# Two decode layers streamed through SBUF: slots of 512 KB in place of 1 MB, half of one head's values kept, second-layer queries taken head by head

## The chip, the cores and the metric

One core of one Trainium2 chip. The time is the device time of one execution in microseconds (us). Ratios are the mean time of one kernel's fast runs over that of the other's in the same rounds, so they are not quite the ratio of the medians that are quoted beside them. The kernel before was run again beside every group of kernels; its median moved between 1197.8 and 1201.7 us from chip to chip, so kernels of different groups are compared by their ratios to it.

In the profiles PE is TensorE, PEld its weight load, DVE VectorE, ACT ScalarE, POOL GpSimd, and SP the engine that issues the loads. The granted clock (PEclk) is the share of TensorE's full clock that a stretch had. An eviction is a copy of TensorE's results into SBUF.

## The reference

Two layers with the same weights and the same caches. Each is grouped-query attention of one new token over 4096 cached positions (16 query heads on 8 key/value heads of width 256), then a small MLP block, for a batch of 8:

```python
B, Sq, D = 8, 1, 448
Hq, Hkv, Sk, Dh = 16, 8, 4096, 256
# k_cache, v_cache: (B, Hkv, Sk, Dh) bf16, 134 MB each
x = x + _A_ref(_layernorm(x), A_k_cache, A_v_cache, A_wq, A_wo)
x = x + _B_ref(_layernorm(x), B_w1, B_w2, B_w3, B_w4)
x = x + _A_ref(_layernorm(x), A_k_cache, A_v_cache, A_wq, A_wo)   # the same caches again
x = x + _B_ref(_layernorm(x), B_w1, B_w2, B_w3, B_w4)
```

Keys and values of one pair (batch element, head) are 2 MB each. Layer 2 of a batch element cannot start before all eight heads of layer 1 and the MLP are done. Whatever is not still in SBUF by then is read from HBM a second time.

## The kernel before

It keeps the keys of five heads of a batch element (10 MB) from layer 1 to layer 2, and streams everything else through the rest of its 15 slots of 1 MB. Keys are transposed on TensorE; scores, softmax and values follow; the values of a pair come one pair later (LAG). A small list scheduler in the kernel takes each operation's estimated duration and fixes the order of every engine's instructions ahead of time. On the chip each engine follows that order.

```python
HALVES = 15          # slots of 1 MB
KEEP_K = 5           # heads whose keys stay
KEEP_V = 0
...
def load_half(cache, b, h, half):
    i = free_slots.pop(0)
    slot_n[i] += 1
    src = cache[b, h].rearrange("(m s) d -> m (s d)", m=P)[:, half * 4096:(half + 1) * 4096]
    dma("kv", slot_ap(i, 0, 4096), src, 1 << 20, slot_sem[i], 16 * slot_n[i],
        [("s", i, j) for j in range(4)], loads[0])
...
# in pair(): per half j: load K, 4 transposes (TensorE) with evictions, 2 groups of score matmuls;
# the slot is free after the last score of the half; V likewise after its last value matmul
```

Between the layers of batch element b stands `mid`: MLP, norm, and the queries of layer 2. The first head's queries are computed and copied alone, the other seven together:

```python
groups = [[heads[0]], heads[1:]]
for gr in groups:
    for h in gr:  pe(... q_mms of head h ...)          # 16 matmuls a head
    for h in gr:  dv(... copy psC to q2T of head h ...)
```

The order of pairs around it, which hides part of `mid` behind two filler heads of the next batch element:

```python
for b in range(B):
    mid(b, l2_heads[0], l2_heads + free_heads)
    layer1(b + 1, free_heads[:NFILL])        # 2 filler heads, beside mid
    layer2(b, l2_heads[:2])                  # heads 7 and 6: keys already in SBUF
    layer1(b + 1, free_heads[NFILL:])
    layer2(b, l2_heads[2:])
    layer2(b, free_heads)
    layer1(b + 1, kept_heads)                # (edge cases cut)
```

## Time and profile before

| | before |
|---|---|
| median of 4 runs | 1197.81 us |
| span of the profiled run | 1196.5 us |
| bytes moved by all queues | 466.5 MB |
| TensorE busy | 84% |

Three lines of the page of the kernel before: the span; each engine's busy time with its share and instructions; and the load queue with its packets, MB and share of 16 engines' span.

```profile
span 1196.5 us, 46172 instructions
PE 1005.6 (84%) x21301; PEld 861.9 (72%) x21301; DVE 509.1 (43%) x1632; ACT 274.3 (23%) x847; POOL 97.9 (8%) x270
q1 hardware_dynamic: 69344, 463.58, 96.1%
```

The load queue is busy nearly all the time, so the loads are the first suspect. Where are they not at full rate? Below are windows of the kernel before: first ten microseconds of the plateau, then stretches of 8 us from the end of layer 1 of the fourth batch element (at 547.4 us). The columns are the stretch, its length, the busy time of each engine with its instructions, the granted TensorE clock, the DMA share, and GB/s.

```profile
core 0: us, PE busy (x) PEld busy (x) DVE busy (x) ACT busy (x) POOL busy (x), PEclk, DMA share, GB/s
480.00:490.00 10.00, 9.32 (x183) 8.09 (x182) 4.73 (x12) 3.58 (x9) 0.75 (x2) 1.00 1.01 419
547.40:555.40 8.00, 8.00 (x160) 7.91 (x158) 5.43 (x19) 2.93 (x5) 0.00 (x0) 1.00 0.99 393
555.40:563.40 8.00, 8.00 (x191) 7.63 (x188) 4.59 (x17) 1.94 (x7) 0.75 (x2) 1.00 0.84 289
563.40:571.40 8.00, 5.82 (x205) 5.17 (x201) 3.20 (x23) 0.65 (x4) 0.75 (x2) 0.91 0.95 355
571.40:579.40 8.00, 7.34 (x164) 6.08 (x165) 2.24 (x8) 1.23 (x5) 0.75 (x2) 0.66 0.86 314
579.40:587.40 8.00, 7.28 (x185) 6.57 (x182) 4.03 (x11) 1.73 (x6) 0.75 (x2) 1.00 1.00 416
```

On the plateau the loads run at 415 to 420 GB/s. After the layer change they sag to 289 GB/s, come back, and sag again to 314. In the first two stretches of 8 us TensorE is busy all of the time, and so, nearly, is its weight load (PEld): 7.91 and 7.63 us. The Trainium skill (Perfetto Trace Analysis, Identifying the Most-Contended Engine) calls matmul busy time a poor measure of how near TensorE is to its limit and asks for its arithmetic rate and the weight-load share; in these two stretches busy time and weight load say the same. The second sag is not the same case: there TensorE is busy 7.34 us and its weight load 6.08, at a granted clock of 0.66. The load queue's own waits in the kernel before, between 122 and 140 us (layer change): who issues, whom it waited for, total, times, longest.

```profile
engine line waited for: us in total, times, longest us
SPq L441 <- PE psS L697: 14.6, 3, 6.7
SPq L441 <- PE psS L737: 4.1, 2, 3.7
```

The queue waits for slots that score (L697) and value matmuls (L737) have yet to free. From the chain of work that ended last, around that change, as start, duration, what:

```profile
138.53 0.43 PE psC L594 x16
138.96 0.54 PE psW L775 x20
139.50 2.83 PE psC L594 x107
142.33 2.29 issue
144.61 0.31 PE psC L594 x5
144.92 2.57 PE psS L697 x64
147.49 1.81 PE psS L737 x32
```

L594 is a query matmul, L697 a score, L775 the output projection. The scores of the first second-layer head (x64) stand behind all 128 query matmuls and an idle of 2.29 us marked "issue" (TensorE waited for nothing that the profile names).

From the packets of a trace I count the bytes that arrive in each stretch, and call *loss* the time by which they fall short of 417.4 GB/s, the plateau of the kernel before. The stretches are set by the moment X at which VectorE writes the last sum of layer 1 of a batch element (the layer change). "Ahead" is X-24 to X, "first dip" X to X+24, "late" X+24 to X+64; each is summed over the eight layer changes. "Rest" is the plateau between them. The time of the bytes and all losses add up to the span by construction:

```
           span = bytes at 417.4 + start + ahead + first dip + late + rest + end
before   1196.5 =        1117.7  +   7.1 +   0.2 +      38.9 + 13.5 +  0.4 + 18.7
```

So 52.6 us are lost around the eight layer changes, 6.6 us at each.

### The profile page before, as it was taken

To read this page: it belongs to the slowest core of one execution; us is meant where nothing else is said; L and a number is where in the kernel's file an instruction comes from. 1 tells how busy PE (TensorE), PEld (TensorE's weight loads), DVE (VectorE), ACT (ScalarE), POOL (GpSimd) and SP (SyncE) were. 2 spreads that over 40 slices of the span, in tenths; PEclk is the share of its full clock that TensorE was granted. 3 is DMA by queue.
4 is the path that set the end of the run, shared out by engine and by line. 5 is a ranking of instruction groups with operands and counts; after the bars stand their busy time and mean duration, and the time that the engine had idled before them with its cause. 6 is when DMAs were issued, how large, how long until landed. Compare 5 with 4: busy or idle time off the path is not lost.

```text
span 1196.5 us, 46172 instructions
## 1 busy us (share of the span) xinstructions
PE 1005.6 (84%) x21301; PEld 861.9 (72%) x21301; DVE 509.1 (43%) x1632; ACT 274.3 (23%) x847; POOL 97.9 (8%) x270
## 2 busy tenths in 40 slices
PE   4878889889898887999789797888888888789787
PEld 4766877778677776777677686776877677678665
DVE  3433435444344443445344343444434453345333
ACT  0222213221132211332123211232223221132121
POOL 0000010000110011000110001000010000100110
PEclk9998889998899988999899988999889997899888
DMA  9999899999999999999999989999999999999893
GB/s 348 409 398 418 320 413 416 417 414 348 417 416 418 385 372 417 418 416 359 390 416 417 418 325 401 417 415 418 346 417 417 417 399 350 417 417 366 345 415 155
DMA packets 69536, 466.52 MB, mean 390 GB/s; under 512 B 7120, under 2 KB 13152, under 8 KB 13664
## 3 DMA queue, kind: packets, MB, share of 16 engines
q1 hardware_dynamic: 69344, 463.58, 96.1%
q8 instruction: 167, 2.74, 0.9%
q14 instruction: 25, 0.20, 0.0%
HBM read 463.54 MB, written 0.01 MB: 387 GB/s over the span
## 4 chain that ended last, share of the span: by engine, by line
PE 53%; DMA 34%; DVE 5%; issue 4%; SPq 3%; POOL 1%; ACT 0%
DMA kv<-in_A_v_cache_dram 20%; PE psT L805 18%; PE psS L697 14%; DMA kv<-in_A_k_cache_dram 14%; PE psS L737 8%; PE psW L775 4%; SPq L441 3%; PE psT L941 2%; DVE oS L751 2%; DVE oS L749 2%; PE psC L640 1%; PE psS L759 1%; PE psC L594 1%; PE psC L534 1%; PE psC L616 1%
## 5 line engine op out<-in xcount | busy, mean ns | idle before, releaser
L805 PE MATMUL psT<-ident_f,kv 128*128 128x128 f32 x2816 | 383.4, 284 | 11.4 <-DMA kv<-in_A_k_cache_dram 8.3
L805 PEld LDWEIGHTS psT<-ident_f,kv 128*128 128x128 f32 x2816 | 315.3, 145 | 25.6 <-DMA kv<-in_A_k_cache_dram 13.7
L813 DVE COPY kv<-psT 128x512 f32<-128x512 f32 x379 | 260.4, 691 | 171.2 <-PE psT L805 168.4
L814 ACT COPY kv<-psT 128x512 f32<-128x512 f32 x325 | 190.3, 586 | 517.9 <-PE psT L805 517.6
L737 PE MATMUL psS<-kv,pT 128*2 128x256 bf16 x4096 | 167.4, 289 | 45.2 <-DMA kv<-in_A_v_cache_dram 38.5
L697 PE MATMUL psS<-q2T,kv 128*128 128x48 bf16 x4096 | 145.6, 192 | 23.0 <-issue 22.8
L717 ACT ACTIVATE pT<-psS,nb 128x32 bf16<-128x32 f32 x256 | 73.2, 296 | 365.0 <-DVE nb L711 365.0
L697 PEld LDWEIGHTS psS<-q2T,kv 128*128 128x128 bf16 x4096 | 133.7, 103 | 31.7 <-issue 29.4
L697 PE MATMUL psS<-q1T,kv 128*128 128x48 bf16 x4096 | 143.2, 183 | 5.4 <-issue 4.9
L697 PEld LDWEIGHTS psS<-q1T,kv 128*128 128x128 bf16 x4096 | 130.1, 97 | 22.8 <-issue 17.6
L737 PEld LDWEIGHTS psS<-kv,pT 128*2 128x2 bf16 x4096 | 78.9, 85 | 75.5 <-DMA kv<-in_A_v_cache_dram 45.0
L709 POOL PARTITION_ALL_REDUCE gm<-pm x128 | 45.4, 354 | 893.5 <-DVE pm L707 845.6
L707 DVE TENSOR_REDUCE pm<-psS 128x2 f32<-128x64 f32 x128 | 28.7, 224 | 182.9 <-PE psS L697 182.2
L941 PE MATMUL psT<-ident_b 128*128 128x256 bf16 x614 | 100.3, 288 | 1.9 <-issue 1.9
L759 PEld LDWEIGHTS psS<-sel,oS 128*128 128x128 bf16 x512 | 23.9, 98 | 105.6 <-DVE oS L751 103.8
L775 PEld LDWEIGHTS psW<-oT,wo_sb 128*128 128x128 bf16 x2560 | 79.9, 97 | 23.2 <-DVE oT L765 11.9
L759 PE MATMUL psS<-sel,oS 128*128 128x2 bf16 x512 | 32.4, 167 | 74.7 <-DVE oS L751 67.7
L775 PE MATMUL psW<-oT,wo_sb 128*128 128x24 bf16 x2560 | 90.0, 183 | 6.0 <-issue 5.0
L749 DVE CAST oS<-psS 128x256 bf16<-128x256 f32 x128 | 54.1, 423 | 74.7 <-PE psS L737 72.3
L941 PEld LDWEIGHTS psT<-ident_b 128*128 128x128 bf16 x614 | 49.6, 100 | 22.9 <-issue 17.6
L722 POOL PARTITION_ALL_REDUCE Db<-rs x128 | 51.1, 399 | 173.4 <-ACT pT L717 173.4
L751 DVE TENSOR_TENSOR oS<-psS,oS 128x256 bf16<-128x256 f32 x128 | 54.3, 424 | 3.3
(83 smaller groups left out, 461.2 us busy)
## 6 DMA issues: line engine op xcount, KB each, us to landing
kv<-in_A_v_cache_dram SPq DMA_DIRECT2D x256, 1024.0 KB, 17.9
kv<-in_A_k_cache_dram SPq DMA_DIRECT2D x176, 1024.0 KB, 20.9
wo_sb<-in_A_wo_dram SPq DMA_DIRECT2D x1, 3584.0 KB, 32.9
wq_sb<-in_A_wq_dram SPq DMA_DIRECT2D x3, 1024.0 KB, 11.3
w_sb<-in_B_w_dram SPq DMA_DIRECT2D x1, 1568.0 KB, 23.8
w_sb<-in_B_w_dram SPq DMA_DIRECT2D x3, 448.0 KB, 24.4
wqx_sb<-in_A_wq_dram SPq DMA_DIRECT2D x2, 256.0 KB, 14.9
w3x_sb<-in_B_w_dram SPq DMA_DIRECT2D x2, 112.0 KB, 20.1
```

The lines of the kernel that those rows point to most:

```text
L697: last = t.matmul(ps[:, 2 * i:2 * i + 2 * REP], a[:, c:256:2], bcast(rhs(c), REP, 1), start=(c == 0), stop=(c == 1))
L717: return a.activation(pT[nr][:, :, :].rearrange("p i j -> p j i")[:, jj, :], sview[:, jj, :], ACT.Exp, bias=nb[nr][:, jj:jj + 1], scale=IN ...
L722: plan.op("pool", lambda gp: gp.partition_all_reduce(Db[nr][:, :], rs[nr][:, :], P, RO.add), 0.5, "sum", rd=[("rs", nr, 0), ("rs", nr, 1)] ...
L737: last = t.matmul(ps[g4:g4 + 2, PV0:PV0 + DH], pT[nr][:, i, :], slot_ap(s_, s * 256, 256), start=(i < 4), stop=(i >= 28), skip_group_check ...
L749: plan.op("dve", lambda v: v.tensor_copy(oS[:, 0, :], po), 0.36, "o", rd=[("pv", par, x) for x in range(4)], wr=["oS0"], banks=[bk], prio=hi)
L751: plan.op("dve", lambda v: v.tensor_tensor(oS[:, 1, :], po, oS[:, 0, :], ALU.subtract), 0.36, "o", rd=["oS0"] + [("pv", par, x) for x in r ...
L759: last = t.matmul(ps[:, PV1 + 2 * c:PV1 + 2 * c + 2], oS[:, w, c * P:(c + 1) * P], sel[:, :], start=(w == 0), stop=(w == 1))
L775: last = t.matmul(psW[:, mt * YW:(mt + 1) * YW], dup(wo_sb, 2 * (2 * h + j) + c, mt), bcast(oT[nr][:, c, j:j + 1], YW, 1), start=(k == 0), ...
L805: last = t.transpose(psT[bank][:, s * P:(s + 1) * P], src, ident_f[:, :])
L813: return e.tensor_copy(dst, psT[bank][:, :])
L814: return e.copy(dst, psT[bank][:, :])
L941: last = t.matmul(psT[bank][:, 256 * i:256 * i + 256], ident_b[:, :], bcast(ident_b[:, :], 2, 1), start=True, stop=True)
```

## The change

The intent: read less (half of one head's values stays, 1 MB per batch element), use the slots in finer pieces where they are scarce and in bigger loads where many are free, and let the first layer-2 scores start earlier. The diff is shortened; words in brackets and comments are mine.

```diff
-HALVES = 15
+QUARTERS = 30
-KEEP_V = 0
+KEEP_V = 2
+MARGIN4, MARGIN2 = 16, 8
+QFIRST = 8
...
+    def grab(n):      # 4, 2 or 1 neighbouring slots, oldest first, if enough others are free
+        rank = {q: k for k, q in enumerate(free_slots)}
+        for k, margin in ((4, MARGIN4), (2, MARGIN2), (1, 0)):
+            if k > n:
+                continue
+            best = None
+            for q in range(0, QUARTERS - k + 1, k):
+                if all(q + x in rank for x in range(k)):
+                    r = max(rank[q + x] for x in range(k))
+                    if r < len(rank) - margin and (best is None or r < best[0]):
+                        best = (r, q)
...
+    def load(cache, b, h, units):    # one DMA and one semaphore for each group of slots grabbed
...
-        for j in range(2):           # halves of 1 MB
+        for u in range(4):           # quarters of 512 KB: loaded, transposed, scored, freed
...
-            for gr in groups: (queries of a group, then its copies)
+        for h in heads:
+            second_queries(b, h, None)      # 16 matmuls, then the copy, head by head
...
-        mid(b, l2_heads[0], l2_heads + free_heads)
+        order2 = l2_heads + free_heads
+        mid(b, order2[:QFIRST])             # QFIRST = 8: all heads, so none is left to spread
+        q_todo[b] = order2[QFIRST:]
```

The edit also gives the scheduler another estimate of a load's duration: the same for 1 MB (2.38 us), 1.22 in place of 1.19 us for 512 KB, 4.70 in place of 4.77 for 2 MB.

More of the change, by code (lines that the diff above doesn't have):

```diff
@@ L346, in bass_interleave_layers__gqa_block_cached__mixer_s_mlp__decode_kernel @@
     plan = Plan()
-    half_b = 8192
-    high0 = 229344 - HALVES * half_b
-    kv = nc.alloc_sbuf_tensor_at("kv", [P, HALVES * half_b // 2], bf, offset=high0)
+    high0 = 229344 - QUARTERS * 4096
+    kv = nc.alloc_sbuf_tensor_at("kv", [P, QUARTERS * 2048], bf, offset=high0)
     cursor = [16512]
@@ L420, in bass_interleave_layers__gqa_block_cached__mixer_s_mlp__decode_kernel, with slot_ap @@
     psW = nc.alloc_psum_tensor("psW", [P, 512], f32)
-    def slot_ap(i, a, n):
-        return kv[:, i * 4096 + a:i * 4096 + a + n]
+    def slot_ap(q, a, n):
+        return kv[:, q * 2048 + a:q * 2048 + a + n]
     sems = {e: nc.alloc_semaphore(f"s_{e}") for e in ("pe", "dve", "act", "pool")}
-    slot_sem = [nc.alloc_semaphore(f"s_slot{i}") for i in range(HALVES)]
-    slot_n = [0] * HALVES
+    slot_sem = [nc.alloc_semaphore(f"s_slot{i}") for i in range(QUARTERS)]
+    slot_n = [0] * QUARTERS
     def bcast(ap, shape, axis):
@@ L435, in bcast, with dma @@
         return bass.AP(tensor=ap.tensor, offset=ap.offset, ap=dims)
-    RATE = 440e3
-    def dma(name, dst, src, nbytes, sem, val, wr, at):
-        plan.op("sp", lambda eng: eng.dma_start(dst, src), nbytes / RATE, name, wr=wr, prio=at,
+    FASTER = 1.05
+    def dma(name, dst, src, nbytes, sem, val, wr, at, row=8192):
+        us = nbytes / 16 / 26.88e3 + nbytes / row / 16 * 0.008
+        plan.op("sp", lambda eng: eng.dma_start(dst, src), us / FASTER, name, wr=wr, prio=at,
                 dma=(sem, val))
@@ L450, in bass_interleave_layers__gqa_block_cached__mixer_s_mlp__decode_kernel @@
     loads = [0]
-    def load_half(cache, b, h, half):
-        i = free_slots.pop(0)
-        slot_n[i] += 1
-        src = cache[b, h].rearrange("(m s) d -> m (s d)", m=P)[:, half * 4096:(half + 1) * 4096]
-        dma("kv", slot_ap(i, 0, 4096), src, 1 << 20, slot_sem[i], 16 * slot_n[i],
-            [("s", i, j) for j in range(4)], loads[0])
-        loads[0] += 1
-        return i
-    free_slots = list(range(HALVES))
+    def grab(n):
[9 more added lines that the diff above has]
+                        best = (r, q)
+            if best is not None:
+                got = [best[1] + x for x in range(k)]
+                for q in got:
+                    free_slots.remove(q)
+                return got
+        raise AssertionError("no slot")
+    def load(cache, b, h, units):
+        out = {}
+        units = list(units)
+        while units:
+            run = 1
+            while run < len(units) and units[run] == units[0] + run:
+                run += 1
+            got = grab(run)
+            n, q, u = len(got), got[0], units[0]
+            slot_n[q] += 1
+            src = cache[b, h].rearrange("(m s) d -> m (s d)", m=P)[:, u * 2048:(u + n) * 2048]
+            dma("kv", slot_ap(q, 0, n * 2048), src, n << 19, slot_sem[q], 16 * slot_n[q],
+                [("s", x, j) for x in got for j in range(2)], loads[0], row=n * 4096)
+            sizes[n] = sizes.get(n, 0) + 1
+            loads[0] += 1
+            for x in range(n):
+                out[u + x] = got[x]
+            units = units[n:]
+        return out
+    sizes = {}
+    free_slots = list(range(QUARTERS))
     YB = ["yb"]
@@ L657, in bass_interleave_layers__gqa_block_cached__mixer_s_mlp__decode_kernel @@
     store = {}
+    KEPT_K = {h: range(4) for h in range(HKV - KEEP_K, HKV)}
+    KEPT_V = {HKV - 1: range(4 - KEEP_V, 4)}
     done = {}
@@ L678, in pair, with sc @@
             qk = [("q2", b, h)]
-        ks = [None, None] if kept_k is None else list(kept_k)
-        vs = [None, None] if kept_v is None else list(kept_v)
-        kept = [ks[j] is not None for j in range(2)]
-        for j in range(2):
-            if ks[j] is None:
-                ks[j] = load_half(A_k_cache, b, h, j)
-            if not kept[j]:
-                for pc in range(4):
-                    transpose_piece(ks[j], pc)
-            for qd in range(2):
-                def sc(t, j=j, qd=qd, s_=ks[j]):
-                    last = None
-                    for s in range(8 * qd, 8 * qd + 8):
-                        i = 16 * j + s
-                        for c in range(2):
-                            a = slot_ap(s_, s * 256, 256)
-                            last = t.matmul(ps[:, 2 * i:2 * i + 2 * REP], a[:, c:256:2],
-                                            bcast(rhs(c), REP, 1), start=(c == 0), stop=(c == 1))
-                    return last
-                plan.op("pe", sc, (0.022 * 16 + 0.06, 32 * REP / 1200 + 0.01, 32 * REP), "sc", rd=qk + [("s", ks[j], 2 * qd), ("s", ks[j], 2 * qd + 1)],
-                        wr=[("sc", par, x) for x in range(2 * j + qd, 4)], banks=[bk])
-            if not keep_k[j]:
-                free_slots.append(ks[j])
+        ks, vs = dict(kept_k), dict(kept_v)
+        fresh = [u for u in range(4) if u not in ks]
+        ks.update(load(A_k_cache, b, h, fresh))
+        for u in range(4):
+            if u in fresh:
+                for pc in range(2):
+                    transpose_piece(ks[u], pc)
+            def sc(t, u=u, q=ks[u]):
+                last = None
+                for s in range(8):
+                    i = 8 * u + s
+                    for c in range(2):
+                        a = slot_ap(q, s * 256, 256)
+                        last = t.matmul(ps[:, 2 * i:2 * i + 2 * REP], a[:, c:256:2],
+                                        bcast(rhs(c), REP, 1), start=(c == 0), stop=(c == 1))
+                return last
+            plan.op("pe", sc, (0.022 * 16 + 0.06, 32 * REP / 1200 + 0.01, 32 * REP), "sc",
+                    rd=qk + [("s", ks[u], 0), ("s", ks[u], 1)],
+                    wr=[("sc", par, x) for x in range(u, 4)], banks=[bk])
+            if u not in keep_k:
+                free_slots.append(ks[u])
         hi = g - 10 ** 5
@@ L726, in back, with pv @@
         def back():
-            for j in range(2):
-                if vs[j] is None:
-                    vs[j] = load_half(A_v_cache, b, h, j)
-                for qd in range(2):
-                    def pv(t, j=j, qd=qd, s_=vs[j]):
-                        last = None
-                        for s in range(8 * qd, 8 * qd + 8):
-                            i = 16 * j + s
-                            g4 = 32 * (i % 4)
-                            last = t.matmul(ps[g4:g4 + 2, PV0:PV0 + DH], pT[nr][:, i, :],
-                                            slot_ap(s_, s * 256, 256), start=(i < 4), stop=(i >= 28),
-                                            skip_group_check=True, tile_position=(0, g4))
-                        return last
-                    plan.op("pe", pv, (0.25, 0.46, 512), "pv",
-                            rd=[("pT", nr, 0), ("pT", nr, 1), ("s", vs[j], 2 * qd),
-                                ("s", vs[j], 2 * qd + 1), ("pz", par)],
-                            wr=[("pv", par, x) for x in range(2 * j + qd, 4)], banks=[bk])
-                if not keep_v[j]:
-                    free_slots.append(vs[j])
+            fresh_v = [u for u in range(4) if u not in vs]
+            vs.update(load(A_v_cache, b, h, fresh_v))
+            for u in range(4):
+                def pv(t, u=u, q=vs[u]):
+                    last = None
+                    for s in range(8):
+                        i = 8 * u + s
+                        g4 = 32 * (i % 4)
+                        last = t.matmul(ps[g4:g4 + 2, PV0:PV0 + DH], pT[nr][:, i, :],
+                                        slot_ap(q, s * 256, 256), start=(i < 4), stop=(i >= 28),
+                                        skip_group_check=True, tile_position=(0, g4))
+                    return last
+                plan.op("pe", pv, (0.25, 0.46, 512), "pv",
+                        rd=[("pT", nr, 0), ("pT", nr, 1), ("s", vs[u], 0), ("s", vs[u], 1),
+                            ("pz", par)],
+                        wr=[("pv", par, x) for x in range(u, 4)], banks=[bk])
+                if u not in keep_v:
+                    free_slots.append(vs[u])
             po = ps[:, PV0:PV0 + DH]
@@ L788, in back @@
                rd=["psW", sk], wr=[dk] + (["x3all"] if dk == ok and layer else []), banks=["W"], name="acc", prio=hi)
-            store[layer, b, h] = ([ks[j] if keep_k[j] else None for j in range(2)],
-                                  [vs[j] if keep_v[j] else None for j in range(2)])
+            store[layer, b, h] = ({u: ks[u] for u in keep_k}, {u: vs[u] for u in keep_v})
         pend.append(back)
@@ L817, in transpose_piece, with mid, second_queries @@
         a.tbank = v.tbank = bank
-    def mid(b, first_head, heads):
+    def mid(b, heads):
         mlp(x1T[:, :, b:b + 1], ("x1", b), 1, x2T[:, :, b:b + 1], [("x2", b)])
         norm(x2T[:, :, b:b + 1], ("x2", b), 1, False)
+        for h in heads:
+            second_queries(b, h, None)
+    def second_queries(b, h, prio):
         q = q2T[b % 2]
-        groups = [[heads[0]], heads[1:]]
-        for gr in groups:
-            for h in gr:
-                pe(lambda t, h=h: q_mms(t, range(4 * h, 4 * h + 4), 1, False), 16, rd=YB + WQ,
-                   wr=["psC"], banks=["C"])
-            lo, hi = min(gr), max(gr)
-            for h in gr:
-                dv(lambda v, h=h: v.tensor_copy(
-                    q[:, 4 * h:4 * h + 4].rearrange("p (c j) -> p c j", c=2),
-                    psC[:, 4 * h * QW:(4 * h + 4) * QW:QW].rearrange("p (j c) -> p c j", c=2)),
-                   rd=["psC"], wr=[("q2", b, h)], banks=["C"])
+        pe(lambda t: q_mms(t, range(4 * h, 4 * h + 4), 1, False), 16, rd=YB + WQ,
+           wr=["psC"], banks=["C"], prio=prio)
+        dv(lambda v: v.tensor_copy(
+            q[:, 4 * h:4 * h + 4].rearrange("p (c j) -> p c j", c=2),
+            psC[:, 4 * h * QW:(4 * h + 4) * QW:QW].rearrange("p (j c) -> p c j", c=2)),
+           rd=["psC"], wr=[("q2", b, h)], banks=["C"], prio=prio)
     dma_once("x", [(x_row[:, 0:D], A_x[:, 0, :], 7168)], ["xr0"], 0)
@@ L876, in first_queries @@
                dur=0.3, rd=["psC"], wr=[("q1T", c)], banks=["C"])
-    no = [False, False]
-    yes = [True, True]
     free_heads = list(range(HKV - KEEP_K))
@@ L885, in layer1 @@
         for h in heads:
-            kk = h in kept_heads
-            nv = KEEP_V if h == HKV - 1 else 0
-            keep_v = [nv > 1, nv > 0]
-            pair(0, b, h, None, None, yes if kk else no, keep_v)
+            pair(0, b, h, {}, {}, KEPT_K.get(h, ()), KEPT_V.get(h, ()))
     def layer2(b, heads):
         for h in heads:
+            todo = q_todo.get(b, [])
+            for h2 in todo[:1 + (h in todo)]:
+                second_queries(b, h2, len(plan.ops))
+                todo.remove(h2)
             kk, kv = store.pop((0, b, h))
-            pair(1, b, h, kk, kv, no, no)
+            pair(1, b, h, kk, kv, (), ())
+    q_todo = {}
     load_wq()
```

## The prediction

> **What bounds it now.** The loads. On the page, queue 1 is busy for 96.1% of 16 engines' span and moves 463.6 MB; TensorE is busy 84%. In ten-microsecond windows the plateau is 415 to 419 GB/s, so 466.5 MB (all queues) need about 1118 us of the 1196.5. The other 78: start about 7, end about 19, and eight dips, one per batch element, when the layer-1 result goes through the MLP to the layer-2 queries. From 120 to 150 us the windows read 351, 283 and 324 GB/s: about 7 us lost, some 50 over eight. There the load queue waits for slots (between 122 and 140 us, 14.6 us on score and 4.1 on value matmuls), and its loads land 5.7 us after issue (27 on the plateau, where many queue). Ten of 15 slots hold kept keys; five stream.
>
> **What the change does.**
> 1. Bytes: for each of 8 batch elements half a head's values is kept, 8 loads of 1 MB less: 8.39 MB at 417 GB/s = -20 us, all on the bound.
> 2. Load sizes: the built program has 112 loads of 2 MB, 132 of 1 MB and 136 of 512 KB in place of 432 of 1 MB. A packet (one partition's row) took a median of 313 ns for 8192 B and 140 ns for 3584 B, so about 5 ns is fixed. Estimated rates: 407, 418 and 422 GB/s for 512 KB, 1 and 2 MB. Net -2 us. The Trainium skill (DMA: Bandwidth & Descriptors, Rules for kernel authors) asks for at least 1 MiB per DMA; the small ones fall in the dips.
> 3. Slots: 22 of 30 kept, so 4 MB streams through the dip instead of 5. Alone that costs up to 2.5 us per dip. Against it, slots come free in smaller pieces; in the new instruction order both filler heads' values (64 value matmuls) are consumed before or among the queries; before, 32.
> 4. Queries: all eight heads are still computed up front (the limit is 8), but scores of the first kept head start after 32 query matmuls; before they stood behind all 128 (2.83 us of matmuls, then 2.29 us idle marked "issue", 139.5 to 144.9 us in the chain). Its key slots come free 3 to 5 us earlier. The price: a TensorE to VectorE round trip per head.
>
> I expect each dip to fall from about 7 to 4 or 5 us: -20 us in all.
>
> **Not helped.** The start (two 2 MB key loads precede wq, so first queries 5 us later) and the end (the last 2 MB of values has one semaphore, so all 32 value matmuls, 1.8 us, follow it): +3 us.
>
> **Sum.** -20 - 2 - 20 + 3 = -39: **1158 us**, range 1142 to 1176. Faster by over 2%: 0.85; within 2%: 0.14; slower: 0.01.
>
> **What would show it.** Queue 1 moves 455.2 MB; plateau windows stay 415 to 420; dips lose 3 to 5 us; second-layer scores begin after the first query groups; TensorE's share rises to about 87%.
>
> **What would make it wrong.** If the smaller stream starves the queue (dips of 8 us, or new ones while the last kept heads load), only the bytes' 20 us are left, or less. If 512 KB loads run below 400 GB/s, or 2 MB loads stall TensorE by arriving whole, the gain halves. If the copies' round trips lengthen the query chain beyond 3 us, item 4 reverses.

## The result, and the profile after

1180.19 us median of 4 runs (1177.3 to 1183.0) against 1197.81 (1197.2 to 1198.5). The ratio is 0.9853, 95% interval 0.9825 to 0.988: the change gains 17.6 us where 39 were predicted, and the time lies above the stated range.

The page of the kernel after, the same lines:

```profile
span 1175.4 us, 45862 instructions
PE 1002.4 (85%) x21205; PEld 858.9 (73%) x21205; DVE 529.1 (45%) x1653; ACT 263.2 (22%) x826; POOL 97.9 (8%) x270
q1 hardware_dynamic: 61856, 455.19, 95.8%
```

455.19 MB, as predicted; TensorE's share is 85%, not 87. The windows of the kernel after: the plateau, then from the end of layer 1 of the fourth batch element (at 542 us).

```profile
core 0: us, PE busy (x) PEld busy (x) DVE busy (x) ACT busy (x) POOL busy (x), PEclk, DMA share, GB/s
480.00:490.00 10.00, 8.99 (x170) 7.98 (x169) 5.30 (x13) 2.40 (x7) 0.75 (x2) 1.00 1.01 423
542.00:550.00 8.00, 8.00 (x147) 7.91 (x145) 5.55 (x21) 3.48 (x9) 0.53 (x2) 1.00 0.87 308
550.00:558.00 8.00, 8.00 (x211) 7.05 (x208) 4.12 (x16) 1.45 (x6) 0.98 (x3) 1.00 0.73 227
558.00:566.00 8.00, 7.00 (x216) 5.73 (x214) 3.67 (x22) 0.65 (x4) 0.75 (x2) 1.00 1.01 385
566.00:574.00 8.00, 5.20 (x157) 4.74 (x156) 1.28 (x8) 0.65 (x4) 0.75 (x2) 0.79 1.00 408
574.00:582.00 8.00, 8.00 (x131) 7.29 (x119) 4.01 (x9) 2.34 (x4) 0.00 (x0) 0.79 0.99 420
582.00:590.00 8.00, 6.40 (x202) 4.74 (x198) 3.10 (x14) 1.29 (x8) 1.50 (x4) 1.00 0.91 350
```

The plateau is faster (423 GB/s). The first dip is deeper (308 and 227 where there were 393 and 289), comes back sooner, and the second sag is gone (408 and 420). But 40 us after the layer change stands a new one: 350 GB/s at 582 to 590 us. The page's list of loads in the kernel after (issuer, count, size of one, median us from issue to landing):

```profile
kv<-in_A_v_cache_dram SPq DMA_DIRECT2D x64, 2048.0 KB, 16.6
kv<-in_A_k_cache_dram SPq DMA_DIRECT2D x48, 2048.0 KB, 22.4
kv<-in_A_v_cache_dram SPq DMA_DIRECT2D x86, 1024.0 KB, 19.7
kv<-in_A_k_cache_dram SPq DMA_DIRECT2D x46, 1024.0 KB, 25.6
kv<-in_A_v_cache_dram SPq DMA_DIRECT2D x68, 512.0 KB, 7.4
kv<-in_A_k_cache_dram SPq DMA_DIRECT2D x68, 512.0 KB, 11.6
```

And the chain of waits in the kernel after, where the queries of the first layer change stand (L628 query, L731 score):

```profile
138.28 0.51 PE psC L628 x16
138.79 0.23 PE psT L977 x2
139.02 0.03 issue
139.04 0.58 PE psC L628 x16
139.62 0.81 PE psS L731 x32
140.43 0.41 PE psC L628 x16
140.84 0.38 PE psS L731 x15
141.22 2.02 issue
143.25 0.60 PE psS L731 x17
```

This part went as predicted. The first scores (x32) follow 32 query matmuls. Over the first seven changes they start 19.4 us after the layer change (23.6 before, mean of eight: 19.9 and 23.6), and the 64th begins after 22.7 us on average in place of 27.6. The idle marked "issue" (2.02 us) is still there, now inside the first head's scores. The packets of the instruction queue tell more of it: each of TensorE's idles of over 0.9 us marked "issue" (23 before, 22 after) ended 1.2 to 1.6 us after a 16 KB packet of that queue did. Of the 126 other idles of that length 6 did so. So these idles very likely wait for instructions; no run varied it. The sum of losses:

```
           span = bytes at 417.4 + start + ahead + first dip + late + rest + end
before   1196.5 =        1117.7  +   7.1 +   0.2 +      38.9 + 13.5 +  0.4 + 18.7
after    1175.4 =        1097.5  +   6.0 +   3.8 +      41.7 + 12.2 -  3.8 + 17.9
```

The bytes give 20.2 us, as predicted. The plateau gives 4.2. Around the layer changes, where I had expected 20 us less, 57.7 us are lost in place of 52.6. That is the missing part.

### The profile page after: what moved, and what is told of

Its sections match the earlier page's. It is cut to its first block, busy times and chain, and to the rows that moved or that the text cites. A ratio compares the mean times of both kernels' runs of the same rounds, so it can differ in the third digit from the quotient of the medians.

```text
span 1175.4 us, 45862 instructions
## 1 busy us (share of the span) xinstructions
PE 1002.4 (85%) x21205; PEld 858.9 (73%) x21205; DVE 529.1 (45%) x1653; ACT 263.2 (22%) x826; POOL 97.9 (8%) x270
## 3 DMA queue, kind: packets, MB, share of 16 engines
q1 hardware_dynamic: 61856, 455.19, 95.8%
## 4 chain that ended last, share of the span: by engine, by line
PE 61%; DMA 28%; issue 6%; DVE 5%; ACT 0%; POOL 0%; SPq 0%; POOLq 0%
PE psT L838 22%; DMA kv<-in_A_k_cache_dram 17%; PE psS L731 16%; DMA kv<-in_A_v_cache_dram 11%; PE psS L771 9%; PE psW L809 4%; PE psC L628 2%; PE psT L977 2%; DVE oS L783 2%; DVE oS L785 2%; PE psC L568 1%; PE psS L793 1%; PE psC L674 1%; PE psC L650 1%; DVE oT L799 0%
## 5 line engine op out<-in xcount | busy, mean ns | idle before, releaser
L838 PE MATMUL psT<-ident_f,kv 128*128 128x128 f32 x2816 | 390.5, 289 | 9.5 <-DMA kv<-in_A_k_cache_dram 9.2
L846 DVE COPY kv<-psT 128x512 f32<-128x512 f32 x400 | 275.3, 691 | 162.3 <-PE psT L838 158.8
L838 PEld LDWEIGHTS psT<-ident_f,kv 128*128 128x128 f32 x2816 | 326.8, 148 | 22.6 <-DMA kv<-in_A_k_cache_dram 15.6
L847 ACT COPY kv<-psT 128x512 f32<-128x512 f32 x304 | 178.2, 587 | 462.5 <-PE psT L838 462.3
L771 PE MATMUL psS<-kv,pT 128*2 128x256 bf16 x4096 | 173.8, 289 | 37.0 <-DMA kv<-in_A_v_cache_dram 22.3
L731 PE MATMUL psS<-q2T,kv 128*128 128x48 bf16 x4096 | 143.0, 190 | 21.3 <-issue 20.3
L731 PEld LDWEIGHTS psS<-q2T,kv 128*128 128x128 bf16 x4096 | 131.3, 101 | 29.1 <-issue 27.7
L731 PE MATMUL psS<-q1T,kv 128*128 128x48 bf16 x4096 | 142.8, 184 | 2.8 <-issue 1.9
L731 PEld LDWEIGHTS psS<-q1T,kv 128*128 128x128 bf16 x4096 | 129.7, 97 | 21.2 <-issue 15.6
L793 PE MATMUL psS<-sel,oS 128*128 128x2 bf16 x512 | 32.3, 167 | 67.0 <-DVE oS L785 66.5
L977 PE MATMUL psT<-ident_b 128*128 128x256 bf16 x518 | 85.6, 285 | 1.8 <-issue 1.8
L977 PEld LDWEIGHTS psT<-ident_b 128*128 128x128 bf16 x518 | 40.8, 100 | 16.1 <-issue 12.0
```

What stands on the lines that cost most here:

```text
L731: last = t.matmul(ps[:, 2 * i:2 * i + 2 * REP], a[:, c:256:2], bcast(rhs(c), REP, 1), start=(c == 0), stop=(c == 1))
L771: last = t.matmul(ps[g4:g4 + 2, PV0:PV0 + DH], pT[nr][:, i, :], slot_ap(q, s * 256, 256), start=(i < 4), stop=(i >= 28), skip_group_check= ...
L793: last = t.matmul(ps[:, PV1 + 2 * c:PV1 + 2 * c + 2], oS[:, w, c * P:(c + 1) * P], sel[:, :], start=(w == 0), stop=(w == 1))
L838: last = t.transpose(psT[bank][:, s * P:(s + 1) * P], src, ident_f[:, :])
L846: return e.tensor_copy(dst, psT[bank][:, :])
L847: return e.copy(dst, psT[bank][:, :])
```

## The experiments

Seventeen kernels ran; all gave a correct result by the comparison with the reference. Each was timed in five rounds, the last two in three.

### Which part of the change does what

**b_keepv1**: the kernel before with one half slot of values kept. The bytes alone.

```diff
-KEEP_V = 0
+KEEP_V = 1
```

> The kernel before, with one of the 15 half slots (1 MB, half of one head's values) kept per batch element: the bytes alone, 8 loads of 1 MB less, and four half slots that stream through the dip instead of five. Capacity theory (each dip lasts as long as the streaming slots let it, so 1 MB less costs 1.5 to 2.5 us per dip): the 20 us of bytes are mostly given back, 1188 to 1198 us, and the loss around each layer change rises from about 6.5 to 8 or 9 us. Rival (capacity costs little, since the bytes that are kept need not come): 1176 to 1181 us, loss per layer change unchanged.

Measured: 1196.53 us, ratio 0.9965 (0.9946 to 0.9983). Of 20 us of bytes only 4 are left. Windows of b_keepv1 from the end of layer 1 of its fourth batch element (columns as above):

```profile
547.10:555.10 8.00, 8.00 (x150) 7.93 (x150) 5.43 (x20) 2.94 (x5) 0.00 (x0) 1.00 0.85 333
555.10:563.10 8.00, 8.00 (x196) 7.71 (x193) 4.47 (x16) 1.94 (x7) 0.75 (x2) 1.00 0.72 243
563.10:571.10 8.00, 6.18 (x209) 5.53 (x207) 3.33 (x24) 0.65 (x4) 0.75 (x2) 0.88 0.94 365
571.10:579.10 8.00, 7.22 (x169) 5.84 (x170) 2.15 (x8) 1.23 (x5) 0.75 (x2) 0.70 0.85 301
```

The same four stretches read 393, 289, 355 and 314 in the kernel before. The loss around the layer changes is 70.7 us, 18.1 more than before, 2.3 us a change. The capacity theory holds.

**b_14**: the kernel before with one slot fewer and nothing kept.

```diff
-HALVES = 15
+HALVES = 14
```

> The kernel before with 14 half slots in place of 15: the same bytes, four streaming slots in the dip. Capacity theory: about 2 us more per dip, 1208 to 1218 us. Rival: within 5 us of before.

Measured: 1218.44 us, ratio 1.0145 (1.0124 to 1.0166), 70.1 us lost around the changes. The same 17.5 us more without any other part of the change: a streaming megabyte is worth nearly what a kept megabyte saves.

**b_q**: the kernel before with its queries copied head by head.

```diff
-        groups = [[heads[0]], heads[1:]]
-        for gr in groups: (queries of the group; then its copies)
+        for h in heads:
+            (16 query matmuls of head h; its copy)
```

> The kernel before with the second-layer queries copied head by head, nothing else. If the early start of the second layer's scores ends the dip sooner (as predicted), each dip loses 1 to 2 us less: 1180 to 1190 us. Rival (the early release of key slots brings no load forward, or the round trips of the copies cost as much): 1194 to 1200 us, with scores starting 3 to 4 us earlier all the same.

Measured: 1188.05 us, ratio 0.9897 (0.9878 to 0.9917). The late loss falls from 13.5 to 2.0 us; the first dip hardly moves (38.9 to 38.4). So the early scores do what was predicted, 12 us in all, and they act on the second sag, not on the first.

**a_oldq**: the kernel after with the old grouping (the same edit the other way).

> The kernel after with the old grouping of the second-layer queries (first head alone, then seven together). If the early start is worth 1 to 2 us per dip: 1189 to 1197 us. Rival: 1178 to 1184 us.

Measured: 1190.85 us, ratio 0.9919 (0.9899 to 0.994), against 0.9853 of the whole change. The late loss rises from 12.2 to 21.5 us. The gain of the queries is there in both kernels.

**a_v0**: the kernel after without kept values.

```diff
-KEEP_V = 2
+KEEP_V = 0
```

> The kernel after without the kept half of the values: the bytes of before, 5 MB streaming through the dip in 512 KB slots. Capacity theory: the loss around each layer change falls by about 2 us against after (from about 7 to 5), 16 us in all, against 20 us more bytes: 1181 to 1187 us, so that keeping the values is worth only some 3 us. Rival (capacity is not what the kept values cost in the after kernel, whose slots are finer): 1195 to 1202 us.

Measured: 1190.52 us, ratio 0.992 (0.9902 to 0.9938): between the two expectations. The loss around the changes falls from 57.7 to 49.3 us, 8.4 us for 20 us more bytes. In the kernel after the kept values are worth some 8 us; in the kernel before, 4.

**h_qv**: both edits of before together, kept values and head-by-head queries, but slots and loads of 1 MB: the change without its small slots.

> The kernel before with the kept half of the values and the queries copied head by head, but still 15 half slots and 1 MB loads: the change without its slots of 512 KB. If the parts add as the single ones did (bytes and capacity together -0.35%, queries -1.03%), the ratio is 0.986, as the whole change's 0.985, and the smaller slots are worth nothing: 1180 to 1187 us. If the smaller slots hold back the loss of capacity, as predicted (about 1 us per dip, and 2 us of load sizes), this one is 10 us slower than after: 1189 to 1195 us.

Measured: 1187.21 us, ratio 0.9902 (0.9876 to 0.9928), so the small slots with their load sizes are worth about 0.5%, 6 us, and the truth lies between the two expectations. The sums show where they act:

```
           bytes + start + ahead + first dip + late + rest + end
h_qv     1097.6  +   6.6 +   0.2 +      56.9 +  3.6 +  0.4 + 19.3
after    1097.5  +   6.0 +   3.8 +      41.7 + 12.2 -  3.8 + 17.9
```

Small slots do shorten the first dip, by 15.2 us over eight. 8.6 us come back late, 3.6 ahead of the dip. What remains for them is 3 us around the changes and 4.2 on the plateau.

The four kernels with head-by-head queries make a table of the other two edits (ratio to before, loss around the changes in us):

| | slots of 1 MB | slots of 512 KB |
|---|---|---|
| no values kept | 0.9897, 40.6 (b_q) | 0.9920, 49.3 (a_v0) |
| half a head's kept | 0.9902, 60.7 (h_qv) | 0.9853, 57.7 (after) |

With slots of 1 MB the kept values are worth nothing that can be seen (0.9897 and 0.9902); with slots of 512 KB, some 8 us. Small slots give 3.0 us around the changes where a megabyte is kept, and lose 8.7 there where none is. These are single traces, and 3.0 is within their scatter (see All runs). Still, what small slots do around the changes is at most to ease the loss of capacity; alone they gain nothing.

The same stretches from the packets, as a mean rate over the first seven layer changes, in GB/s, in bins of 4 us from X-8 to X+52 (the last column begins at X+48):

```
X+        -8  -4   0   4   8  12  16  20  24  28  32  36  40  44  48
before   416 418 418 353 288 259 269 406 344 359 413 421 419 417 417
h_qv     416 418 315 263 214 258 299 409 423 415 416 416 417 417 416
after    408 408 380 331 236 239 389 402 397 383 411 423 307 406 425
a_no4    409 400 339 322 228 233 397 384 383 417 418 418 416 416 417
e36      408 408 390 338 239 228 403 399 373 412 418 420 416 322 384
```

### What gives the relief back: load sizes

**a_no4**: the kernel after with no load of 2 MB.

```diff
-MARGIN4, MARGIN2 = 16, 8
+MARGIN4, MARGIN2 = 99, 8
```

> The kernel after with no loads of 2 MB (1 MB at most). Large-load theory (a 2 MB load waits until four slots are free, which makes the new short dip some 40 us after the layer change): that dip goes, about 1 us per batch element, but the plateau falls from about 424 back to 418 GB/s, about 6 us: 1175 to 1181 us. Rival (the new dip has another cause): the dip stays and the time rises to 1184 to 1188 us.

Measured: 1184.53 us, ratio 0.9873 (0.9847 to 0.9898). In the mean rate over the first seven changes, the 307 GB/s at 40 to 44 us after the change becomes 416; the late loss falls from 12.2 to 3.3 us. But the plateau's gain goes too (rest from -3.8 to 0.5), and the first dip rises from 41.7 to 47.1, which I had not expected. The time is in the rival's range, though the rival's reason is denied: the dip went.

**a_m20_12**: larger margins, so smaller loads in and after the dip.

```diff
-MARGIN4, MARGIN2 = 16, 8
+MARGIN4, MARGIN2 = 20, 12
```

> The kernel after with larger margins for the double and quadruple slots (20 and 12 for 16 and 8), so that loads in and just after the dip are smaller (216 loads of 512 KB more or less in place of 136, 87 of 2 MB in place of 112; about 4 us more transfer time by packet times). Large-load theory: the third dip shrinks and the first one by some tenths: 1173 to 1180 us. Rival (packet cost decides): 1182 to 1187 us.

Measured: 1186.36 us, ratio 0.9892 (0.987 to 0.9913): slower, though packets explain only 4 us. First dip 43.4, late 13.2: no gain in either place.

**a_no42**: every load of 512 KB (both margins 99).

> The kernel after with every load of 512 KB: the finest use of the slots. The plateau falls to about 407 GB/s by packet times, 25 us more than after. If finer loads turn slots over faster, the dips' loss falls by 1.5 us each or more, 1185 to 1195 us. If a load's fixed time sets the turnover in the dip (1 MB loads that find the queue nearly empty land 5.2 us after issue, 512 KB loads 4.9), the loss per dip falls by less than 0.7 us: 1198 to 1206 us.

Measured: 1206.5 us, ratio 1.0065 (1.0035 to 1.0094). The plateau, in a window of a_no42:

```profile
480.00:490.00 10.00, 10.00 (x206) 8.83 (x205) 5.80 (x16) 2.88 (x8) 0.76 (x2) 1.00 1.03 407
```

407 GB/s for 512 KB, where the same window reads 419 for 1 MB before and 423 after, most of it 2 MB. In the traces a packet of 4, 8 and 16 KB takes a median of 161, 313 and 614 ns: by their differences a fixed 9 to 12 ns for each. The Trainium skill (DMA: Bandwidth & Descriptors, Measured) gives 341 GB/s for 1 MB issued from GpSimd and a rule of at least 1 MiB; in a queue that always holds several loads the step from 1 MB to 512 KB costs 2.9%. The loss of 72.0 us counts against 417.4 GB/s; against this kernel's own 407 it is about 56, so the dips hardly fell (57.7 in the kernel after). A load's time has a part that does not shrink. 1 MB loads issued at most 3 us ahead of the previous load's landing (the queue nearly empty) land 5.2 us after issue (115 of them in the traces of before, b_keepv1, b_14 and b_q), 512 KB loads 4.9 (21 of them in the six first traces with small slots). The transfer itself is 2.5 and 1.3 us. The skill's page (Anatomy of one DMA) puts a fixed 2.0 us on a load issued by another path; here it is about 2.7 us for 1 MB. Part of the 5.2 and 4.9 is waiting behind the load before; the one 1 MB load of the 115 that found the queue empty landed after 4.9.

**c24_36**: load sizes by place, with half of the queries really spread.

```diff
-QFIRST = 8
+QFIRST = 4
+        top = 1 if since[0] < 24 else 2 if since[0] < 36 else 4    # slots loaded since the change
-            if k > n:
+            if k > min(n, top):
```

> The kernel after with four heads' queries up front and with load sizes set by place: 512 KB for the first 24 slots loaded after each layer change, at most 1 MB for the next 12, then as before. Large-load theory: the third dip, 40 us after the change, goes (1 us per batch element) and the first dip falls by 0.3 to 0.5 us each; packets cost 4 us more: 1168 to 1176 us. Rival (sizes in the dip matter no more than their packets cost): 1180 to 1186 us.

Measured: 1179.8 us, ratio 0.9846 (0.9819 to 0.9874): level with the whole change. Two things differ from it at once, sizes and queries; a_q2 below has the queries alone.

**c24**: the same without the cap of 1 MB between 24 and 36 slots.

> The same with 2 MB loads allowed again right after the first 24 slots. If the third dip comes from the first 2 MB loads that wait for four slots, it is there again and this one is 2 to 6 us slower than the version that has 1 MB loads in that place; if not, it is 1 us faster (fewer packets).

Measured: 1189.07 us, ratio 0.9906 (0.9879 to 0.9934), 9 us slower than c24_36, more than the theory allows. In its mean rate there is no sag at 40 to 44 us (425 GB/s), but one at 16 to 32 us (303 to 348). But c24_36 has nearly the same sag there (305 to 361), so it does not account for the 9 us. Between the two profiled runs lie 10.7 us: 5.6 around the changes and 4.8 at the end of the kernel (23.7 us lost there, 18.9 in c24_36). So the time agrees with the theory and the place does not.

**e36**: the cap of 1 MB for the first 36 slots alone, with all queries up front. Only the first three 2 MB loads of a batch element are split.

```diff
+        top = 2 if since[0] < 36 else 4
-            if k > n:
+            if k > min(n, top):
```

> The kernel after with loads of at most 1 MB for the first 36 slots loaded after each layer change: only the first three 2 MB loads of each batch element are split, the loads in the first dip are the same. If those loads, each waiting for four slots, make the dip 40 us after the change: the mean rate there rises from about 307 to over 390 GB/s, the ratio to before falls from 0.985 to about 0.980 (6 us of dip, less 1 us of packets). If not: 0.985 to 0.988 and the dip stays.

Measured: 1175.67 us, ratio 0.978 (0.9757 to 0.9803). The time is even better than expected, but not for the whole reason. Windows of e36, 32 to 48 us after the layer change of the fourth batch element:

```profile
571.40:579.40 8.00, 6.40 (x127) 5.73 (x126) 3.82 (x9) 2.62 (x6) 0.40 (x1) 0.98 1.01 420
579.40:587.40 8.00, 6.58 (x154) 4.88 (x146) 2.36 (x10) 1.20 (x8) 1.11 (x3) 0.59 0.90 342
```

The sag did not go; it moved. In the mean rate it stood at 40 to 44 us after the change (307 GB/s) in the kernel after, and stands at 44 to 48 us (322) in e36. Both times a 2 MB load is late. The load queue's own waits in the kernel after, between 575 and 590 us:

```profile
SPq L444 <- PE psS L771: 9.3, 2, 8.6
```

Over the first seven changes the third 2 MB load of the kernel after, 39 to 42 us after the change, was issued 7.0 to 9.1 us after the load before it; in e36 the first one, at 44 to 48 us, 7.3 to 10.8. That supports the cause (a 2 MB load is issued only when all four slots are free, so the queue runs short once while the loads change size) and denies the remedy. It is not the whole cause: in c24_36 the first 2 MB load waits as long (6.6 to 10.4 us) and the rate falls only to 408. The sums hold only 3.1 us of the gain (57.7 to 54.6); the profiled run of e36 is just 1.1 us shorter than that of after, since its end takes 2.4 us more (20.3 and 17.9). The rest of the 0.7% is not explained by these traces.

### What the order of work does

**a_q2**: queries really spread, two heads up front.

```diff
-QFIRST = 8
+QFIRST = 2
```

> The kernel after with two heads' queries up front and the other six really spread among the later heads. If TensorE's query work (some 3 us per batch element) delays the second head's scores and with it the releases: 0.5 to 1 us less per dip, 1170 to 1177 us. Rival (what matters is the first head's start alone, which is unchanged): 1178 to 1184 us.

Measured: 1176.72 us, ratio 0.9812 (0.9791 to 0.9832). The late loss falls from 12.2 to 6.0 us; the 128th score (end of the second head) comes 29.5 us after the change in place of 31.1.

**e36_q2**: both edits.

> The same with two heads' queries up front and the rest spread. If both gains stand side by side: ratio to before 0.975 to 0.979, faster than both kernels by over 2%. If they are one gain (both remove the dip at 40 us): 0.980 to 0.983, as spreading alone (0.981).

Measured: 1181.02 us, ratio 0.9831 (0.9809 to 0.9853). The gains do not add; this is slower than e36.

**v0_c24**: no kept values, 512 KB loads for the first 24 slots after the change.

> The kernel after without kept values (5 MB streams through the dip) and with 512 KB loads for the first 24 slots after each layer change. If small loads turn the streaming slots over faster, the loss in the first dip (up to 24 us after the change) falls from 5.5 us to 4 or less and the ratio from 0.992 to 0.985 or less. If the order in which TensorE takes the work, or the fixed time of a load, holds the dip: the loss stays within 0.5 us of 5.5 and the ratio is 0.990 to 0.995.

Measured: 1197.54 us, ratio 0.9973 (0.995 to 0.9997). A telling miss. Small loads do turn the slots over faster: against a_v0 the first dip falls from 43.1 to 27.5 us. All of it and more comes back late: from 3.2 to 27.6. The second layer's first scores come 23.4 us after the change where a_v0 has 21.3, and the 64th at 28.0 where it has 25.1. In both, TensorE is busy 8.0 of the first 8 us. The order did change: ahead of the first scores stand 63 value matmuls in place of 32, but 112 scores in place of 128 and fewer transposes. TensorE is busy 21.1 us there in place of 19.9, at a mean granted clock of 0.92 in place of 0.96 (means over the first seven changes); busy time multiplied by the clock is 19.5 and 19.2. So most of the lateness is not more work in the order, and why the loss comes back stays open.

**x_notr** and **h_notr**: TensorE relieved. The key transposes of the two filler heads are left out, in the kernel after and in h_qv. The arithmetic is then wrong; the result still passed the comparison, whose tolerance does not see these heads.

```diff
-                for pc in range(2):
+                for pc in range(0 if raw[0] and layer == 0 else 2):     # raw: the filler heads
                     transpose_piece(ks[u], pc)       # h_notr: the same in the half-slot code
```

> The kernel after without the key transposes of the two filler heads in each layer change (64 of TensorE's matmuls of 112 ns, about 7 us, and their evictions; loads, slots and waits as before; the result is wrong on purpose). If TensorE's work paces the dip: the loss per layer change falls from 7 us to 4 or less, and the time by 24 us or more, to 1150 us or less. If the slots alone pace it (the chain of small steps from layer 1 to the queries is as long as ever): within 8 us of after, 1172 to 1180.

> The same cut in the version with kept values, head-by-head queries and 1 MB half slots, whose ratio to before is 0.990 with the transposes. If smaller slots were of no use in the dips only because TensorE was full, this one's loss per layer change is 1.5 us or more above that of the cut kernel with 512 KB slots. If smaller slots do nothing for the dips either way: within 0.7 us of it.

Measured: x_notr 1172.07 us, ratio 0.9759 (0.9721 to 0.9797); h_notr 1165.86 us, ratio 0.9713 (0.968 to 0.9746). The first 16 us after the change of the fourth batch element, for h_qv, h_notr and x_notr in turn:

```profile
542.90:558.90 16.00, 16.00 (x347) 15.62 (x346) 10.08 (x38) 4.87 (x12) 0.75 (x2) 1.00 0.75 267
```

```profile
532.70:548.70 16.00, 13.03 (x322) 10.65 (x318) 6.15 (x38) 1.51 (x9) 1.51 (x4) 0.99 1.00 393
```

```profile
536.70:552.70 16.00, 13.55 (x287) 11.22 (x283) 4.25 (x27) 1.51 (x9) 1.51 (x4) 0.75 1.00 379
```

With TensorE busy 13.0 and 13.6 of 16 us and not 16.0, the rate in this stretch goes from 267 to 393 GB/s; in the kernel after the same stretch reads 268 and in x_notr 379. So TensorE's work paces the first part of the dip in both (the cut also takes evictions from VectorE, but at 10.1 of 16 us that engine was not full). But the total does not follow, and x_notr's time is in the range of "the slots alone". h_notr loses 41.4 us around the changes (h_qv 60.7), x_notr still 53.8 (after 57.7): late loss is 13.2, and its second-layer scores start at 21.2 us after the change, later than in the kernel after (19.9). My rival, that small slots were useless only because TensorE was full, gets no support: relieved, the kernel with half slots is the faster of the two.

But the two did not have the same clock. In the lines above x_notr was granted 0.75 and h_notr 0.99. The next 8 us, x_notr first:

```profile
552.70:560.70 8.00, 7.55 (x157) 5.22 (x157) 2.99 (x17) 0.00 (x0) 0.00 (x0) 0.50 0.63 231
```

```profile
548.70:556.70 8.00, 7.56 (x200) 6.15 (x200) 1.82 (x11) 0.65 (x4) 0.75 (x2) 0.50 0.99 363
```

From the change to the first second-layer score, as a mean over the first seven changes, the granted clock was 1.00 in the kernel after and in h_qv, 0.81 in h_notr and 0.68 in x_notr. TensorE's busy time there, multiplied by the clock, is 12.4 us in x_notr and 13.4 in h_notr: the small-slot order has no more work ahead of its scores. So the lower clock is a rival for why they come late, and the pair cannot decide about the small slots. Why the clock was lower is not shown.

### All runs

Loss is the sum of ahead, first dip and late, in us. Bytes at 417.4 GB/s take 1117.7 us without kept values and about 1097.5 with them.

| kernel | median us | ratio to before | first dip | late | loss | rest |
|---|---|---|---|---|---|---|
| before | 1197.81 | 1 | 38.9 | 13.5 | 52.6 | 0.4 |
| after | 1180.19 | 0.9853 | 41.7 | 12.2 | 57.7 | -3.8 |
| b_keepv1 | 1196.53 | 0.9965 | 55.7 | 14.8 | 70.7 | 0.4 |
| b_14 | 1218.44 | 1.0145 | 49.4 | 16.1 | 70.1 | 0.3 |
| b_q | 1188.05 | 0.9897 | 38.4 | 2.0 | 40.6 | 0.4 |
| h_qv | 1187.21 | 0.9902 | 56.9 | 3.6 | 60.7 | 0.4 |
| a_oldq | 1190.85 | 0.9919 | 44.3 | 21.5 | 69.6 | -3.9 |
| a_v0 | 1190.52 | 0.9920 | 43.1 | 3.2 | 49.3 | -4.1 |
| a_no4 | 1184.53 | 0.9873 | 47.1 | 3.3 | 55.8 | 0.5 |
| a_m20_12 | 1186.36 | 0.9892 | 43.4 | 13.2 | 61.4 | -2.5 |
| a_no42 | 1206.50 | 1.0065 | 43.2 | 24.1 | 72.0 | 9.0 |
| c24_36 | 1179.80 | 0.9846 | 42.9 | 12.3 | 58.9 | -3.6 |
| c24 | 1189.07 | 0.9906 | 46.8 | 13.8 | 64.5 | -3.7 |
| a_q2 | 1176.72 | 0.9812 | 43.8 | 6.0 | 55.3 | -3.7 |
| e36 | 1175.67 | 0.9780 | 39.8 | 11.0 | 54.6 | -3.7 |
| e36_q2 | 1181.02 | 0.9831 | 43.1 | 10.4 | 57.5 | -3.4 |
| v0_c24 | 1197.54 | 0.9973 | 27.5 | 27.6 | 59.1 | -4.0 |
| x_notr | 1172.07 | 0.9759 | 36.6 | 13.2 | 53.8 | -3.8 |
| h_notr | 1165.86 | 0.9713 | 32.3 | 8.3 | 41.4 | 0.3 |

Each loss comes from one profiled execution. Single traces and timed means differ by 2 to 5 us (b_keepv1: span 0.5 us below before, timed mean 4 us), so small differences between losses are not evidence. The best correct version is e36, ahead of both kernels: its interval (0.9757 to 0.9803) lies below that of after (0.9825 to 0.988), but it overlaps that of a_q2 (0.9791 to 0.9832).

## Why the prediction was wrong, point by point

- **Bound by loads: right.** Between the changes the loads run at 417 GB/s before and 422 after; what is left of the span is the eight dips, the start and the end.
- **Bytes, -20 us: right.** 20.2 us.
- **Load sizes, -2 us: rates right, net smaller.** The estimated 407, 418 and 422 GB/s were measured as 407, 419 and 423. For 512 KB there was luck in it: the "about 5 ns" of the prediction gives 412, and the packets show 9 to 12 ns. The plateau gains 4.2 us with 2 MB loads, and 3.6 us are lost ahead of the dips, where loads are small.
- **"I expect each dip to fall from about 7 to 4 or 5 us: -20 us in all": the step that failed.** Measured: 5.1 us more. It was the net of three terms, and only the net was put in numbers:
  - *Fewer streaming slots*, "up to 2.5 us per dip": right with slots of 1 MB. 18.1 us by b_keepv1, 17.5 by b_14, 20.1 from b_q to h_qv, so 2.2 to 2.5 a dip. With small slots 8.4 us (a_v0 to after).
  - *Earlier scores*: right in place, and 12 us in all by b_q, 1.5 a dip. I had read "3 to 5 us earlier" from the order; the scores were about 4 us earlier, but a microsecond earlier is not a microsecond of load time.
  - *Small slots*: the largest error. 15.2 us less in the first dip (h_qv to after), of which 12.2 came back ahead of it and late. To reach -20 with the other two terms they had to give 26 net; they gave 3. The terms, with 2.0 us that the first two cost more together than apart: 18.1 - 12.0 + 2.0 - 3.0 = 5.1. Even the gross 15.2 would have made -9, not -20.
- **Why small slots gave their gain back: shown in part.** Shown: loads ahead of the dip are slower (their rate is 405 to 412 GB/s on average there); a sag about 40 us after the change goes when there are no 2 MB loads (a_no4) and moves when they come later (e36); small loads in the dip shorten it, and more than all of it comes back late (v0_c24). Not shown: that this comes from the fixed order on a full TensorE. x_notr and h_notr show that TensorE paces the first 16 us; whether relieving it would rescue the small slots they leave open, since their clocks differ.
- **"Not helped", start and end, +3 us: wrong, small.** Start and end are 1.1 and 0.8 us shorter.
- **Stated as what would make it wrong**: "if the smaller stream starves the queue ... only the bytes' 20 us are left, or less". That came, in a milder form: dips of 7.2 us, not 8, and a new sag after them. A chance of 0.14 was too little for a risk that I had costed at 2.5 us a dip myself.

Still open: why a_no4's first dip grows by 5 us, why c24 lags c24_36 by 9 us, and most of e36's gain over after. Each size edit also reorders TensorE's work, and the granted clock in the dips differs from run to run; these runs cannot part the three.

## What to carry to other kernels

Where a stage starves for slots, count what it can absorb until the next release: keeping data takes slots away from the stream, so price a kept megabyte by its streaming value (of 20 us here 16 to 20 with slots of 1 MB, 8 to 12 with slots of 512 KB) before counting its bytes as gain. An earlier release pays where it ends the wait that ends last, and it may be handed back at the next step: look for the new sag after the old one, and write each term of a net with its own number. With engines that follow a fixed order, change one size at a time, and compare the order that comes out and the granted clock of the stretch.

## What the Trainium skill lacked or had wrong

- DMA: Bandwidth & Descriptors, Measured and Rules for kernel authors: the measured figures are for loads issued from GpSimd, and the rule stops at 1 MiB. The row for 1 MB does not agree with itself: its 6.15 us would be 170 GB/s, not 341. Lacking is how the rate of queued loads from SyncE depends on their size: they ran at 407 GB/s in pieces of 512 KB, 417 to 419 in pieces of 1 MB and 423 where most were 2 MB, one core running. What bigger loads cost is lacking too: a load of several slots waits for the last of them, 8.6 us for one of 2 MB here, and the rate fell to 307 GB/s for 4 us.
- The same page, Anatomy of one DMA: 2.0 us fixed, for the other path. With the queue nearly empty, 1 MB loads from SyncE landed 5.2 us after issue, 2.7 more than their transfer of 2.5.
- Runtime: NRT & Kernel Launch, Instruction fetch mechanics: it says that crossing a 16 KiB block of instructions is mostly hidden. In the kernels before and after, TensorE stands idle for 1 to 3 us, marked "issue", 23 and 22 times, at nearly every layer change (2.29 us and 2.02 at the first one), while the instruction queue moves 167 and 166 blocks of 16 KB in all. Every one of these idles ended 1.2 to 1.6 us after such a block had arrived. So "mostly hidden" agrees in number, but one block in seven was not hidden.
- Perfetto Trace Analysis, Identifying the Most-Contended Engine: no correction. Matmul busy (16.0 of 16 us) and weight-load busy (15.6) agreed in the dip that TensorE paces. They parted in the second sag of the kernel before (7.34 and 6.08 of 8 us).
